# Letting the transposing DMAs run ahead, and two small reorderings, in a layer norm + (S5 state space ∥ SwiGLU) kernel

## The chip, the cores and the metric

One core of one Trainium2 chip. The metric is the device time of one execution in microseconds; each kernel was run several times, and for two kernels that are compared, in alternation on the same chip. The profile gives a span that is about 1.8 us shorter than the metric.

## The reference

The input x has 2048 tokens of 512 elements. All tensors are bf16.

```python
xn = (x - mean(x)) / sqrt(var(x) + 1e-5)                 # over the 512 elements
# S5: a diagonal complex state space over the 2048 tokens
dt = exp(log_dt); Lam = Lambda_re + 1j*Lambda_im; Lam_bar = exp(dt*Lam)
Bu = xn @ (((Lam_bar - 1)/Lam)[:, None] * (B_re + 1j*B_im)).T
h[t] = Lam_bar * h[t-1] + Bu[t]
ssm = 2*real(h @ (C_re + 1j*C_im).T) + xn*Dskip
# SwiGLU, 512 -> 1376 -> 512
ffn = (silu(xn @ w_gate) * (xn @ w_up)) @ w_down
out = x + ssm + ffn
```

## The kernel before

The work is cut into 4 chunks of 512 tokens; a chunk is 4 x tiles of 128 tokens. Chunk 0 is x tiles 0 to 3, chunk 1 is 4 to 7, chunk 2 is 8 to 11, chunk 3 is 12 to 15.

The program first builds a list of tasks with what each reads and writes, and then orders them. TensorE and SP (SyncE, which issues most DMAs) keep the order in which the tasks were added. The orders of ScalarE, VectorE and GpSimd are chosen by a list scheduler before the program is built, from *estimated* durations, and are fixed from then on. Whatever changes an estimated time in the plan can therefore change these three orders, and at run time an engine waits for the next task of its list even if a later one is ready.

```python
_CHAIN = ("pe", "sp")        # in program order; the other engines are ordered by the scheduler
# ... (cut)
# in _schedule: the estimated times of a DMA
        if t.dma:
            issue_done = st + t.est
            xs = max(st + min(t.est, 300.0), dma_free[e])
            dma_free[e] = xs + t.nbytes / (_DMA_BW if e == "sp" else 0.5 * _DMA_BW)
            t.fin = dma_free[e] + _DMA_LAT
            free[e] = issue_done
```

A transposing DMA waits for all DMAs before it, and every later DMA waits for the last transposing one:

```python
        def dma(name, dst, src, writes, nbytes, reads=(), after=(), out_=False, eng="sp", xpose=False, prio=0.0, order=(), **kw):
            after = tuple(after)
            if xpose:
                after = after + tuple(dma_tasks)
                # ... (cut)
            else:
                if xp_state[0] is not None:
                    after = after + (xp_state[0],)
                # ... (cut)

        x_load(0)
        x_load(1)
        act_q = [dma("ld_touch", tch[0:16], wg_v[0:128:8, :, 0:2], [("tch",)], 16 * 16, eng="act")]
        act_q.append(wg_load("a0", 0, 2, eng="act", order=(act_q[-1],)))
        x_load(2)
        act_q.append(wg_load("a1", 2, 3, eng="act", order=(act_q[-1],)))
        wg_load("a2", 3, 4)
        x_load(3)
        pload("ld_ldt", 2, A_log_dt)
        pload("ld_lim", 1, A_Lambda_im)
        pload("ld_lre", 0, A_Lambda_re)
        # ... (cut: w_up, the rest of w_gate, x tiles 4 to 7)
        # later on SP: ld_bre, ld_bim (transposing), the transposes of the normalised x (transposing),
        # ld_cre, ld_cim (transposing), then ld_x8 (x tiles 8 to 11), w_down, ld_x12, ld_dsk
```

The statistics of chunk 2 need x tiles 8 to 11 and go through three engines in four steps: VectorE's `bn_stats` and `bn_aggr`, GpSimd's power for `rstd`, VectorE's `nmr` (mean times rstd, negated), and ScalarE's normalisation `xn8` to `xn11`:

```python
        def ln_apply_act(a0):
            g.add("dve", ... nmr = -mv * rstd ..., name="nmr%d" % a0, est=70)
            for a in range(a0, a0 + 4):
                g.add("act", ... activation(out=xn_sb[:, a % NXN, :], in_=x_sb[:, a, :], func=AF.Identity,
                      scale=rstd[:, a:a + 1], bias=nmr[:, a:a + 1]), name="xn%d" % a, est=710)
```

The same ScalarE also evacuates TensorE's results from PSUM (`u_sb`, `sg`, `uf` in the profile); a bank pair that it hasn't emptied is one that TensorE can't write. VectorE computes, among much else, the C weights `W12` (`W` in the profile) that TensorE needs for the output of chunk 0.

## Time and profile before

Median 179.93 us (179.9 to 180.0, 6 runs). TensorE is nearly always busy:

| what | before | view |
|---|---|---|
| TensorE (PE) busy | 174.4 of 178.1 us, 98% | page |
| VectorE (DVE) busy | 162.3 us, 91% | page |
| ScalarE (ACT) busy | 88.8 us, 50% | page |
| TensorE's longest row without a gap | 7.01 us to 175.77 us | timeline |
| x tiles 8 to 11: issued, landed | 36.79, 40.26 us | timeline and trace |
| last C weight ready, first needed | 73.08, 75.06 us | timeline |

From the page of the kernel before (its lines on busy time and on the chain of work that ended last, by engine and by line):

```profile
span 178.1 us, 2421 instructions
PE 174.4 (98%) x929; PEld 84.1 (47%) x937; DVE 162.3 (91%) x281; ACT 88.8 (50%) x114; POOL 10.3 (6%) x21
...
PE 95%; DVE 2%; DMA 1%; issue 0%; ACT 0%
```

The chain is 95% TensorE: nothing but its own row of matmuls sets the time after start-up. SP's timeline of the kernel before (start us, duration us, then what is issued; the duration is that of the issue, not of the transfer):

```profile
5.81 0.55 SPq L400 DMA_DIRECT2D x_sb<-in_A_x_dram  x1
14.00 2.06 SPq L395 DMA_TRANSPOSE BT<-in_A_B_re_dram  x1
18.54 2.00 SPq L395 DMA_TRANSPOSE BT<-in_A_B_im_dram  x1
22.90 1.78 SPq L395 DMA_TRANSPOSE xnT<-xn_sb  x1
28.54 1.70 SPq L395 DMA_TRANSPOSE hss<-in_A_C_re_dram  x1
32.63 1.97 SPq L395 DMA_TRANSPOSE hss<-in_A_C_im_dram  x1
36.79 0.37 SPq L400 DMA_DIRECT2D x_sb<-in_A_x_dram  x1
```

The gaps between the transposes, 14.00 to 18.54 and so on, are the waits: each starts only when the one before has landed. The first line is x tiles 4 to 7, the last x tiles 8 to 11. The gate weights are issued on ScalarE's queue, behind the touch DMA; its timeline has

```profile
1.23 0.97 ACTq L400 DMA_DIRECT2D wg<-in_B_w_gate_dram  x2
```

What then happens to x tiles 8 to 11 is read from VectorE's timeline, then ScalarE's, then TensorE's (a bracket gives the idle time before an instruction and what ended it):

```profile
40.28 2.47 DVE L479 BATCH_NORM_STATS2 st<-x_sb 128x6 f32<-128x512 bf16 x4 [0.76 <-DMA x_sb<-in_A_x_dram]
...
45.67 0.16 DVE L500 SCALAR_TENSOR_TENSOR nmr<-mv,rstd 128x4 f32<-128x4 f32 x1 [0.86 <-POOL rstd L491]
```
```profile
43.88 1.02 ACT L754 ACTIVATE sg<-pb 128x1024 bf16<-128x1024 f32 x1
45.95 2.93 ACT L503 ACTIVATE xn_sb<-x_sb,nmr,rstd 128x512 bf16<-128x512 bf16 x4 [1.04 <-DVE nmr L500]
48.78 1.00 ACT L810 ACTIVATE uf<-pb 128x1024 bf16<-128x1024 f32 x1
```

### The profile page before, as it was taken

The numbers are of one execution on the slowest core, as the hardware profiler recorded it, in microseconds if no ns is written. First come the engines' busy times: TensorE is split into PE (matmuls) and PEld (weight loads), VectorE is DVE, ScalarE is ACT, GpSimd is POOL, SyncE is SP. The second block draws the span as 40 slices with busy tenths as digits, with TensorE's granted clock in tenths as the row PEclk, the third lists the DMA queues.
The fourth block names the chain that finished last, engine by engine and source line by source line (L and its number), as shares of the span: only waits on it lengthen the run. The fifth ranks groups of instructions, "written<-read, shape, count | busy, mean of one in ns | idle before, by whom it ended". The sixth has DMA issues, their size and how long they took to land.

```text
span 178.1 us, 2421 instructions
## 1 busy us (share of the span) xinstructions
PE 174.4 (98%) x929; PEld 84.1 (47%) x937; DVE 162.3 (91%) x281; ACT 88.8 (50%) x114; POOL 10.3 (6%) x21
## 2 busy tenths in 40 slices
PE   8999999999999999999999999999999999999994
PEld 2794444444444444444444444444444444444743
DVE  2958984889799999989999999999999999999983
ACT  4469999999799948016565651000965620000000
POOL 3023300002200000050000000000000000000000
PEclk9999999999999999999999999999999999999999
DMA  5995593669260000001330000001100000000123
GB/s 168 377 328 117 119 118 74 136 179 346 88 121 0 0 0 0 0 31 61 86 64 0 0 0 4 0 0 59 59 0 4 0 0 0 0 0 4 59 77 100
DMA packets 22978, 12.37 MB, mean 69 GB/s; under 512 B 15192, under 2 KB 22968, under 8 KB 22968
## 3 DMA queue, kind: packets, MB, share of 16 engines
q1 hardware_dynamic: 22472, 11.54, 24.9%
q10 hardware_dynamic: 496, 0.69, 1.1%
q8 instruction: 7, 0.11, 0.3%
q14 instruction: 3, 0.02, 0.0%
HBM read 6.46 MB, written 2.10 MB: 48 GB/s over the span
## 4 chain that ended last, share of the span: by engine, by line
PE 95%; DVE 2%; DMA 1%; issue 0%; ACT 0%
PE pb L742 36%; PE pb L940 21%; PE pb L857 16%; PE pb L953 15%; PE pb L783 3%; PE pb L820 2%; DMA x_sb<-in_A_x_dram 1%; PE pb L830 1%; PE pb L568 1%; DVE xn_sb L514 1%; DVE st L527 0%; DVE st L509 0%; ACT sd L521 0%; DVE mv L519 0%; DVE rstd L530 0%
## 5 line engine op out<-in xcount | busy, mean ns | idle before, releaser
L897 DVE TENSOR_TENSOR_SCAN rot<-sm,car,rot 128x512 bf16<-128x512 f32 x32 | 38.9, 1266 | 0.1
L940 PE MATMUL pb<-wd,hT 128*128 128x512 bf16 (+3 forms) x194 | 38.1, 355 | 0.2
L742 PE MATMUL pb<-xnT,wu 128*128 128x512 bf16 x160 | 37.3, 379 | 0.0
L742 PE MATMUL pb<-xnT,wg 128*128 128x512 bf16 x132 | 31.3, 379 | 0.0
L953 PE MATMUL pb<-W,hss 128*128 128x512 bf16 (+2 forms) x140 | 28.1, 355 | 0.2
L857 PE MATMUL pb<-xnT,BT 128*128 128x512 bf16 x128 | 28.1, 379 | 0.0
L940 PEld LDWEIGHTS pb<-wd,hT 128*128 128x128 bf16 (+1 forms) x198 | 18.5, 98 | 19.9
L742 PEld LDWEIGHTS pb<-xnT,wu 128*128 128x128 bf16 x160 | 15.6, 98 | 18.9 <-issue 0.2
L754 ACT ACTIVATE sg<-pb 128x1024 bf16<-128x1024 f32 x20 | 20.2, 1025 | 8.3 <-PE pb L742 7.2
L810 ACT ACTIVATE uf<-pb 128x1024 bf16<-128x1024 f32 x20 | 20.6, 1029 | 6.8 <-PE pb L742 6.7
L953 PEld LDWEIGHTS pb<-W,hss 128*128 128x128 bf16 x144 | 13.4, 98 | 14.3
L742 PEld LDWEIGHTS pb<-xnT,wg 128*128 128x128 bf16 x132 | 12.7, 98 | 15.7 <-issue 0.8
L857 PEld LDWEIGHTS pb<-xnT,BT 128*128 128x128 bf16 x128 | 12.5, 98 | 15.1
L864 ACT ACTIVATE u_sb<-pb 128x1024 bf16<-128x1024 f32 x16 | 16.4, 1027 | 4.6 <-PE pb L857 4.2
L812 DVE TENSOR_TENSOR hT<-sg,uf 128x1024 bf16<-128x1024 bf16 x20 | 13.5, 682 | 0.8 <-ACT uf L810 0.6
L888 DVE TENSOR_TENSOR rot<-u_sb,cosT 128x2048 bf16<-128x2048 bf16 x8 | 9.7, 1218 | 2.9 <-ACT cosT L703 2.9
L958 DVE TENSOR_TENSOR x_sb<-pb,x_sb 128x512 bf16<-128x512 f32 (+2 forms) x18 | 10.8, 622 | 1.2 <-PE pb L953 1.2
L839 ACT ACTIVATE sg<-pb 96x1024 bf16<-96x1024 f32 x2 | 2.0, 1021 | 17.3 <-PE pb L820 17.3
L503 ACT ACTIVATE xn_sb<-x_sb,nmr,rstd 128x512 bf16<-128x512 bf16 x8 | 5.9, 803 | 9.6 <-DVE nmr L500 9.6
L888 DVE TENSOR_TENSOR rot<-rot,cosT 128x2048 bf16<-128x2048 bf16 x8 | 9.7, 1215 | 0.1
L888 DVE TENSOR_TENSOR rot<-rot,sin 128x2048 bf16<-128x2048 bf16 x8 | 9.7, 1216 | 0.0
L888 DVE TENSOR_TENSOR rot<-u_sb,sin 128x2048 bf16<-128x2048 bf16 x8 | 9.7, 1216 | 0.0
(78 smaller groups left out, 144.3 us busy)
## 6 DMA issues: line engine op xcount, KB each, us to landing
out_dram<-x_sb SPq DMA_DIRECT2D x15, 128.0 KB, 1.7
x_sb<-in_A_x_dram SPq DMA_DIRECT2D x3, 512.0 KB, 7.6
wd<-in_B_w_down_dram SPq DMA_DIRECT2D x1, 1280.0 KB, 7.1
wu<-in_B_w_up_dram SPq DMA_DIRECT2D x1, 768.0 KB, 5.0
wu<-in_B_w_up_dram SPq DMA_DIRECT2D x1, 608.0 KB, 7.1
x_sb<-in_A_x_dram SPq DMA_DIRECT2D x4, 128.0 KB, 3.3
wg<-in_B_w_gate_dram SPq DMA_DIRECT2D x1, 480.0 KB, 6.0
wg<-in_B_w_gate_dram ACTq DMA_DIRECT2D x1, 448.0 KB, 3.8
```

The lines of the kernel that those rows point to most:

```text
L503: g.add("act", lambda e, a=a: e.activation(out=xn_sb[:, a % NXN, :], in_=x_sb[:, a, :], func=AF.Identity, scale=rstd[:, a:a + 1], bias=nmr ...
L742: inst = e.matmul(pbank[0:fs, bk, :].rearrange("p (j t) -> p j t", j=4), lhsT=w[:, kt, i * 128:i * 128 + fs], rhs=xnT[:, c % 2, :, kt, :], ...
L754: g.add("act", lambda e: e.activation(out=sg[rows, sl, 0:n, :].rearrange("p a t -> p (a t)"), in_=pair_f32(rows, bk, 512 * n), func=AF.Sil ...
L810: g.add("act", lambda e: e.activation(out=uf[rows, ul, 0:n, :].rearrange("p a t -> p (a t)"), in_=pair_f32(rows, bk, 512 * n), func=AF.Ide ...
L812: g.add("dve", lambda e: e.tensor_tensor(out=hT[rows, hb, i0:i0 + n, :], in0=sg[rows, sl, 0:n, :], in1=uf[rows, ul, 0:n, :], op=ALU.mult), ...
L857: inst = e.matmul(pbank[:, bk, :].rearrange("p (j t) -> p j t", j=4), lhsT=BT[:, ri, kt, pt * 128:(pt + 1) * 128], rhs=xnT[:, c % 2, :, kt ...
L864: g.add("act", lambda e: e.activation(out=u_sb[:, us].rearrange("p r t -> p (r t)"), in_=pair_f32(slice(0, 128), b0), func=AF.Identity), r ...
L888: tt = lambda out, a, b, op, r, w, nm: g.add("dve", lambda e: e.tensor_tensor(out=out, in0=a, in1=b, op=op), reads=r, writes=w, name="%s_% ...
L897: g.add("dve", lambda e, A0=A0, A1=A1, k=k, ri=ri, pt=pt: e.tensor_tensor_scan(out=A1[:, k, ri, :], data0=rr[:, pt:pt + 1].to_broadcast([1 ...
L940: inst = e.matmul(pbank[:, bk, 0:nc_], lhsT=hT[0:fs, hb, i, lt * 128:(lt + 1) * 128], rhs=wd[0:fs, i, c0:c0 + nc_], start=(i == 0), stop=F ...
L953: inst = e.matmul(pbank[:, bk, 0:nc_], lhsT=hss[:, hb, pt, ri, lt * 128:(lt + 1) * 128], rhs=W12[:, ri, pt, c0:c0 + nc_], start=False, sto ...
L958: g.add("dve", lambda e, bk=bk, a=a, c0=c0, nc_=nc_: e.tensor_tensor(out=x_sb[:, a, c0:c0 + nc_], in0=pbank[:, bk, 0:nc_], in1=x_sb[:, a, ...
```

## The change

Three parts, each meant to start work earlier.

1. Transposing DMAs lose their waits. All are issued by SP, so they stay on one queue.
2. On ScalarE's queue the tiny touch DMA goes, and two parameter loads from SP's queue come in its place, ahead of the gate weights. (`act_table` also loses a bias operand.)
3. On VectorE, the statistics of tile 1's first half come ahead of tile 0's reciprocal.

```diff
@@ transposing DMAs
             if xpose:
-                after = after + tuple(dma_tasks)
 ...
-                if xp_state[0] is not None:
-                    after = after + (xp_state[0],)
@@ ScalarE's queue
-        act_q = [dma("ld_touch", tch[0:16], wg_v[0:128:8, :, 0:2], [("tch",)], 16 * 16, eng="act")]
+        act_q = [pload("ld_ldt", 2, A_log_dt, eng="act")]
+        act_q.append(pload("ld_lim", 1, A_Lambda_im, eng="act", order=(act_q[-1],)))
         act_q.append(wg_load("a0", 0, 2, eng="act", order=(act_q[-1],)))
 ...
-        pload("ld_ldt", 2, A_log_dt)
-        pload("ld_lim", 1, A_Lambda_im)
@@ VectorE, chunk 0
             last = ln_stat0(0, (bn_full(0),))
+            last = bn_half(1, 0, order=(last,))
             for a in range(4):
                 # reciprocal of tile a, first half of tile a ...
-                if a == 0:
-                    last = bn_half(1, 0, order=(last,))
-                    last = ln_half(0, 1, order=(last,))
 ...
-                if a:
-                    last = ln_half(a, 1, order=(last,))
+                last = ln_half(a, 1, order=(last,))
```

(The removal of the now unused names and of `bias=epst[:, 0:1]` in `act_table` is cut.)

More of the change, by code (lines that the diff above doesn't have):

```diff
@@ L331, in bass_parallel_sum__ssm_conv_s5__swiglu_ffn__prompt_kernel @@
         epst = sb("epst", [128, 1], F32)
-        tch = sb("tch", [16, KT, 2], B16)
         praw = sb("praw", [128, 3, PT], B16)
@@ L386, in bass_parallel_sum__ssm_conv_s5__swiglu_ffn__prompt_kernel @@
         wu_v = B_w_up.rearrange("(k p) f -> p k f", p=128)
-        dma_tasks = []
-        xp_state = [None]
         def dma(name, dst, src, writes, nbytes, reads=(), after=(), out_=False, eng="sp", xpose=False, prio=0.0, order=(), **kw):
@@ L402, in dma @@
             t = g.add(eng, fn, reads=reads, writes=writes, name=name, dma=True, after=after, out=out_, est=est, nbytes=nb, prio=prio, order=order)
-            dma_tasks.append(t)
-            if xpose:
-                xp_state[0] = t
             return t
@@ L462, in act_table @@
         def act_table(func, order):
-            g.add("act", lambda e: e.activation(out=sm[:, NSM - 1, 0:1], in_=epst[:], func=func, bias=epst[:, 0:1]), reads=[("epst",)], writes=[("sm", "_warm")],
+            g.add("act", lambda e: e.activation(out=sm[:, NSM - 1, 0:1], in_=epst[:], func=func), reads=[("epst",)], writes=[("sm", "_warm")],
                   name="act_warm", est=1500, order=order)
```

## The prediction

> **What bounds the kernel.** The chain of waits that ended last is 95% TensorE. From 7.01 us to 175.77 us it is one row of matmuls with 0.05 us pauses; the windows table gives TensorE 17.00 of 17.00 us busy in most stretches at a granted clock of 1.00. Before that come about 6.2 us of start-up (first x tile's DMA 0.79 to 3.04, statistics, square root on ScalarE, reciprocal, normalisation of tiles 0 and 1), after it about 2 us of last addition and store. Only the start-up can be shortened, unless a new wait opens later.
>
> **What the change does.**
> 1. Transposing DMAs lose their waits. In the timeline of the DMA queue the B transposes start at 14.0 and 18.54 us, xnT of chunk 1 at 22.9, the C pair at 28.54 and 32.63, x tiles 8 to 11 at 36.79. Each issue takes about 2.0 us and lands 4.1 to 4.5 us after its start; its data flow about 2.2 us. I expect B issued from about 6 us, xnT at about 19.5 (it waits for VectorE), x tiles 8 to 11 at about 25, landed near 29.6 instead of 40.2. All stay on one queue: the Trainium skill, "DMA: Bandwidth & Descriptors", section "Silent corruption: two transposing streams in flight at once", asks for waits only between streams; no run here shows it yet. TensorE reads B first at 24.75 us, 1.85 us after it lands already: no gain. VectorE recovers part of its 4.1 us idle between 25 and 41 us (statistics of chunk 2 fill the 2.85 us wait for the cosine table).
> 2. The 0.41 us touch DMA on ScalarE's queue gives way to two parameter loads (0.37 and 0.25 us on SP). Gate weights and the table load (2.23 us) move about 0.3 us later; the first square root had 0.19 us of slack, so it starts about 0.1 us late. SP gets free about 0.7 us earlier; its loads are limited by bandwidth, so little follows.
> 3. Tile 1's first statistics (0.42 us) move into the 0.36 us in which VectorE waits for the square root. But x tile 1 lands near 4.2 us by the issue table (issued 1.24, about 2.95 us), after the 3.97 us at which it could start; so tile 0's reciprocal slips about 0.1 us. Tile 1's comes about 0.25 us earlier, and the first transpose of tile 1 (now 7.01 us) 0.1 to 0.2 us earlier.
>
> **Sum.** About -0.15 us of 179.94: predicted 179.8 us, 8 in 10 between 179.5 and 180.2. Faster by over 2%: 0.01; within 2%: 0.97; slower: 0.02.
>
> **What would show it.** TensorE's unbroken row starts 0.1 to 0.2 us earlier; B transposes issued near 6 us, landed by 18; VectorE idle in 25 to 41 us cut by over 2 us; TensorE busy time unchanged; hss of the last chunk, now finished at 168.35, finished 2 to 3 us earlier.
>
> **What would make it wrong.** (a) The new VectorE order puts a residual addition and chunk 3's statistics (about 3.6 us) ahead of the C weights W. W ends at 73.0, TensorE needs it at 75.06; I estimate 73.7 to 74, but if x tiles 8 to 11 land after 31 us, TensorE waits up to 1 us. (b) ScalarE waits for chunk 2's statistics amid PSUM evacuations; about 1.4 us of slack. (c) Transposes beside the w_up load delay it past 14.38 us.

## More of the kernel before

```profile
40.38 1.05 PE L830 MATMUL pb<-xnT,wu 128*64 128x512 bf16 x8
41.37 1.90 PE L742 MATMUL pb<-xnT,wg 128*128 128x512 bf16 x8
...
44.83 1.89 PE L742 MATMUL pb<-xnT,wg 128*128 128x512 bf16 x8
...
75.06 5.13 PE L953 MATMUL pb<-W,hss 128*128 128x512 bf16 x22
```

ScalarE waits 1.04 us for `nmr` and then runs four normalisations before its next evacuation, at 48.78; TensorE shows no gap around it. So one wait of about 1 us was already in ScalarE's list and cost nothing.

## The result

| | us, median | range, runs | ratio to before, 95% |
|---|---|---|---|
| before | 179.93 | 179.9 to 180.0, 6 | |
| after | 181.91 | 181.2 to 184.24, 6 | 1.0096 [1.0078, 1.0115] |

The run of 184.24 was slow (clock 0.991) and is left out of the ratio. A ratio here is the mean time of one kernel's fast runs over the mean of the other's fast runs of the same rounds, so it isn't quite the ratio of the medians. The change costs 1%, and the prediction's range (179.5 to 180.2) didn't hold it.

The page of the kernel after, the same lines:

```profile
span 180.1 us, 2416 instructions
PE 175.4 (97%) x937; PEld 84.2 (47%) x937; DVE 161.9 (90%) x281; ACT 87.9 (49%) x114; POOL 10.0 (6%) x21
...
PE 73%; DMA 8%; SPq 6%; DVE 6%; ACT 4%; POOL 2%; issue 1%; ACTq 0%; DVEq 0%
```

The busy times hardly moved. (TensorE's 1 us more is not made of the 8 matmul records that the profile before lacks, 929 against 937: e12 below has all 937, with 174.4 us.) But the chain now passes through a DMA, SP's queue, VectorE, GpSimd and ScalarE before it comes back to TensorE. ScalarE's queue, then SP's timeline, after:

```profile
1.67 0.96 ACTq L394 DMA_DIRECT2D wg<-in_B_w_gate_dram  x2
```
```profile
5.16 1.28 SPq L394 DMA_DIRECT2D x_sb<-in_A_x_dram  x1
6.48 7.72 SPq L391 DMA_TRANSPOSE BT<-in_A_B_re_dram  x1
14.24 3.03 SPq L391 DMA_TRANSPOSE BT<-in_A_B_im_dram  x1
20.16 1.81 SPq L391 DMA_TRANSPOSE xnT<-xn_sb  x1
22.01 2.64 SPq L391 DMA_TRANSPOSE hss<-in_A_C_re_dram  x1
24.69 3.59 SPq L391 DMA_TRANSPOSE hss<-in_A_C_im_dram  x1
28.32 0.58 SPq L394 DMA_DIRECT2D x_sb<-in_A_x_dram  x1
```

Two things to see. The gate weights on ScalarE's queue start 0.44 us later. And x tiles 8 to 11 are issued 8.5 us earlier, but not as early as hoped, since the issues themselves have become long: 7.72, 3.03, 2.64 and 3.59 us where each took 1.7 to 2.1 us before. They landed at 32.74 us (issue to landing 4.4 us). VectorE, ScalarE and TensorE after:

```profile
32.77 2.47 DVE L469 BATCH_NORM_STATS2 st<-x_sb 128x6 f32<-128x512 bf16 x4 [3.65 <-DMA x_sb<-in_A_x_dram]
...
38.76 0.16 DVE L490 SCALAR_TENSOR_TENSOR nmr<-mv,rstd 128x4 f32<-128x4 f32 x1 [1.00 <-POOL rstd L481]
```
```profile
39.01 0.81 ACT L493 ACTIVATE xn_sb<-x_sb,nmr,rstd 128x512 bf16<-128x512 bf16 x1 [4.23 <-DVE nmr L490]
39.73 1.00 ACT L851 ACTIVATE u_sb<-pb 128x1024 bf16<-128x1024 f32 x1
40.63 0.80 ACT L493 ACTIVATE xn_sb<-x_sb,nmr,rstd 128x512 bf16<-128x512 bf16 x1
```
```profile
40.78 1.05 PE L817 MATMUL pb<-xnT,wu 128*64 128x512 bf16 x8 [0.16 <-ACT u_sb L851]
42.40 1.90 PE L729 MATMUL pb<-xnT,wg 128*128 128x512 bf16 x8 [0.56 <-ACT u_sb L851]
...
46.66 1.90 PE L729 MATMUL pb<-xnT,wg 128*128 128x512 bf16 x8 [0.63 <-ACT uf L828]
...
77.04 3.19 PE L940 MATMUL pb<-W,hss 128*128 128x512 bf16 x14
```

The statistics of chunk 2 are now 7.5 us earlier, and yet ScalarE waits four times as long for them, 4.23 us instead of 1.04. The scheduler, which expected x tiles 8 to 11 even earlier (its plan, read by building the kernels again without a chip, has them land at 28.34 us; before, at 38.41), put the normalisations at a much earlier place in ScalarE's list: between the evacuations of `u_sb`. While ScalarE waits for `nmr`, it evacuates nothing, and TensorE runs out of PSUM. Comparing starts of the same matmuls before and after:

| matmul row | before | after | lag | added |
|---|---|---|---|---|
| w_up, 64 wide | 40.38 | 40.78 | 0.40 | 0.23 |
| w_gate | 41.37 | 42.40 | 1.03 | 0.63 |
| w_gate, two rows on | 44.83 | 46.66 | 1.83 | 0.80 |
| first use of W | 75.06 | 77.04 | 1.98 | 0.15 |

The lag at 38.5 us, before the first row of the table, is 0.17 us and comes from start-up (below). The next three rows add 1.67 us (unrounded), the wait for W another 0.15. Their sum, 1.99 us, is the growth of the span (178.1 to 180.1).

The start-up: TensorE begins tile 1's w_gate matmuls at 7.44 us instead of 7.13, because it waits 0.3 us for a part of the gate weights; by 13.5 us 0.17 us of that is left. This is one profile's start: the same first DMAs gave other starts in other runs (see below).

```profile
PEld pb L729 <- ACT u_sb L851: 1.2, 2, 1.0
PEld pb L729 <- ACT uf L828: 1.1, 1, 1.1
...
PEld pb L940 <- DVE W L704: 0.5, 1, 0.5
...
PEld pb L770 <- DMA wg<-in_B_w_gate_dram: 0.3, 1, 0.3
```

These are from the waits view of the kernel after, for TensorE's weight loads (in total, times, longest). None of the four is in the same view of the kernel before.

### The profile page after: what moved, and what is told of

The parts are those of the page before. It is cut to its first block, busy times and chain, and to the rows that moved or that the text cites. A ratio compares the mean times of both kernels' runs of the same rounds, so it can differ in the third digit from the quotient of the medians.

```text
span 180.1 us, 2416 instructions
## 1 busy us (share of the span) xinstructions
PE 175.4 (97%) x937; PEld 84.2 (47%) x937; DVE 161.9 (90%) x281; ACT 87.9 (49%) x114; POOL 10.0 (6%) x21
## 4 chain that ended last, share of the span: by engine, by line
PE 73%; DMA 8%; SPq 6%; DVE 6%; ACT 4%; POOL 2%; issue 1%; ACTq 0%; DVEq 0%
PE pb L729 27%; PE pb L927 21%; PE pb L940 15%; PE pb L844 8%; DMA x_sb<-in_A_x_dram 8%; SPq L391 4%; DVE st L469 3%; SPq L394 2%; ACT xn_sb L493 2%; ACT u_sb L851 2%; POOL rstd L481 1%; PE pb L807 1%; DVE xn_sb L485 1%; DVE hT L799 1%; POOL ve L477 1%
## 5 line engine op out<-in xcount | busy, mean ns | idle before, releaser
L927 PE MATMUL pb<-wd,hT 128*128 128x512 bf16 (+3 forms) x198 | 38.8, 355 | 0.0
L940 PEld LDWEIGHTS pb<-W,hss 128*128 128x128 bf16 x144 | 13.4, 98 | 14.5 <-DVE W L704 0.5
L469 DVE BATCH_NORM_STATS2 st<-x_sb 128x6 f32<-128x512 bf16 x12 | 7.5, 680 | 5.4 <-DMA x_sb<-in_A_x_dram 5.4
```

Source lines behind the costliest of these rows:

```text
L469: return g.add("dve", lambda e, a=a: e.bn_stats(out=st[:, a, :], in_=x_sb[:, a, :]), reads=[("x", a)], writes=[("st", a)], name="bnst%d" % ...
L927: inst = e.matmul(pbank[:, bk, 0:nc_], lhsT=hT[0:fs, hb, i, lt * 128:(lt + 1) * 128], rhs=wd[0:fs, i, c0:c0 + nc_], start=(i == 0), stop=F ...
L940: inst = e.matmul(pbank[:, bk, 0:nc_], lhsT=hss[:, hb, pt, ri, lt * 128:(lt + 1) * 128], rhs=W12[:, ri, pt, c0:c0 + nc_], start=False, sto ...
```

## The experiments

The theory: **the cost is ScalarE's fixed order**. The scheduler planned for x tiles 8 to 11 earlier than they land; ScalarE waits for them in front of evacuations that TensorE needs. The rivals: (R1) the unserialized transposes cost by themselves, by contention or by SP's long issues; (R2) the start-up, that is the later gate weights, costs it all; (R3) VectorE's later C weights W cost it. And, once the place was known: does the *lateness* of the loads cost the time, or the *order* that was made for it?

All 14 experiments gave correct results. The ratio is to the kernel before in the same rounds.

### e1 to e3: each part alone

**e1_transposes_only**: before, with part 1.

```diff
-                after = after + tuple(dma_tasks)
-                if xp_state[0] is not None:
-                    after = after + (xp_state[0],)
```

> Before with nothing but the waits of the transposing DMAs taken away; the scheduler then orders VectorE and ScalarE anew. Theory A (the loss between 38 and 77 us comes with this part, because the new order puts chunk 2's normalisation between PSUM evacuations and x tiles 8 to 11 land too late for it): 180.7 to 181.7 us, x tiles 8 to 11 landing near 32 us, ScalarE waiting 2 to 4 us for nmr, TensorE's start-up unchanged at 7.01 us. Rival (the loss belongs to the start-up parts, whose later loads push everything): within 0.2 us of before.

Measured: 179.91 us, 1.0009 [0.9997, 1.0022]. **A miss** for theory A. ScalarE waits 1.68 us for `nmr` (statistics at 31.79), and none of it reaches TensorE: the waits view shows 0.4 us of TensorE's weight loads on ScalarE, but its matmuls after the wait are as late against the kernel before as those ahead of it (0.06 us).

**e2_ploads_only**: before, with part 2, apart from the bias.

```diff
-        act_q = [dma("ld_touch", ..., eng="act")]
+        act_q = [pload("ld_ldt", 2, A_log_dt, eng="act")]
+        act_q.append(pload("ld_lim", 1, A_Lambda_im, eng="act", order=(act_q[-1],)))
...
-        pload("ld_ldt", 2, A_log_dt)
-        pload("ld_lim", 1, A_Lambda_im)
```

> Before with only the two parameter loads in place of the touch DMA on ScalarE's queue. Theory: gate weights are issued 0.44 us later and the second gate load lands near 7.4 us instead of 5.9, so TensorE waits about 0.3 us for it: 180.1 to 180.3 us. Rival (the start-up loss of the changed kernel comes from VectorE's new order instead): within 0.05 us of before.

Measured: 181.38 us, 1.0082 [1.0069, 1.0095], **a miss** upwards. The smallest part makes most of the loss. x tiles 4 to 7 land near 14.5 us instead of 13.76; the serialized chain behind them shifts (B_re's issue 14.90 instead of 14.00, x tiles 8 to 11 37.97 instead of 36.79); chunk 2's statistics start at 41.56 instead of 40.28, ScalarE waits 2.27 us for `nmr` instead of 1.04, and TensorE waits 0.9 us for the evacuation of `uf` behind it:

```profile
47.26 2.93 ACT L501 ACTIVATE xn_sb<-x_sb,nmr,rstd 128x512 bf16<-128x512 bf16 x4 [2.27 <-DVE nmr L498]
```
```profile
PE pb L740 <- ACT uf L808: 0.9, 1, 0.9
```

From there on TensorE is 1.07 us later than ahead of the wait, against the kernel before; near the end it loses 0.42 us more, waiting for `hss`. ScalarE's order is that of the kernel before; its wait is 1.23 us longer because the statistics come 1.28 us later.

**e3_stats_only**: before, with part 3 (its diff is the last block of the change).

> Before with only the statistics of tile 1 ahead of tile 0's reciprocal. Theory: first transpose of tile 1 at about 6.85 instead of 7.01 us and every later matmul earlier by as much: 179.7 to 179.85 us. Rival (x tile 1 lands too late, about 4.2 us, and holds the reciprocal): 179.95 to 180.2 us.

Measured: 179.99 us, 1.0 [0.9988, 1.0013]. Tile 1's first transpose starts at 6.95 instead of 7.01 us, as part 3 intends, but ScalarE's wait grows to 1.65 us and TensorE waits 0.3 us for `uf`. So the theory's range was **missed**; the time lies in the rival's, but not for the rival's reason.

What follows: R1 falls, the transposes alone cost nothing. Part 2 is the trigger. In e2 the wait is the same one (ScalarE, `nmr`, then an evacuation) in the serialized arrangement, so it doesn't need part 1.

### e4 and e6: the order and the DMAs of part 1, taken apart

In e4 the kernel after issues its DMAs as it does, but the scheduler orders the engines as if the old waits were there. e6 is the reverse: the kernel after's order, with the old waits at run time.

```diff
+            # extra: the waits of the kernel before for this DMA
+            xtra.append((t, extra))
...
+        for t, x in xtra:          # e4 only: plan with the old waits
+            t.deps |= x
         streams = _schedule(g.tasks, engs)
+        for t, x in xtra:          # e4: run without them    (e6: t.deps |= x, run with them)
+            t.deps -= x
```

> The changed kernel, whose DMA waits stay away on the chip, but whose engines' order is made with the old waits in the scheduler's graph, so VectorE and ScalarE keep the old order in chunk 0. Theory A (the compute order causes the loss): TensorE waits nowhere between 14 and 77 us, only the start-up loss of 0.17 us is left: 180.0 to 180.3 us. Rival B (transposing DMAs in flight beside loads hurt by themselves): 181.3 us or more.

Measured: 179.86 us, 0.9996 [0.9984, 1.0008]. The DMAs run as in the kernel after (x tiles 8 to 11 issued at 28.36 us), and ScalarE doesn't wait for `nmr` at all: its normalisations stand late in its list, at 44.82 us, in the order of the kernel before. The expected start-up loss of 0.17 us isn't there (0.02), so the time is below its range.

> The changed kernel's order on every engine, but on the chip the transposing DMAs wait as before. Theory (the landing of x tiles 8 to 11 decides): it lands near 41.5 us instead of 32.7, ScalarE waits 12 to 13 us for nmr, and about 8.5 us more of it reach TensorE: 188 to 191 us. Rival (transposes in flight together cost the time by themselves): 180 to 181 us, as they wait again.

Measured: 190.27 us, 1.0569 [1.0519, 1.0619] (profile at a clock of 0.982). ScalarE waits 13.00 us for `nmr` and TensorE 8.9 us for ScalarE. ScalarE's line, then TensorE's wait:

```profile
47.40 0.81 ACT L501 ACTIVATE xn_sb<-x_sb,nmr,rstd 128x512 bf16<-128x512 bf16 x1 [13.00 <-DVE nmr L498]
```
```profile
PE pb L825 <- ACT u_sb L859: 8.9, 1, 8.9
```

What follows: the same DMAs with another order lose nothing (e4); the same order with later DMAs loses 8.4 us more than the kernel after (e6). The mechanism is shown, and R2 falls: e4 keeps the changed start of the DMAs, part 2's too, and is as fast as before.

### e5: the late input earlier

The kernel after with x tiles 8 to 11 issued ahead of the two C transposes; the orders of the other engines stay.

```diff
         streams = _schedule(g.tasks, engs)
+        q = streams["sp"]
+        x8 = next(t for t in q if t.name == "ld_x8")
+        q.remove(x8)
+        q.insert(next(k for k, t in enumerate(q) if t.name == "ld_cre"), x8)
```

> The changed kernel, every engine's order as it is, but the load of x tiles 8 to 11 is issued ahead of the two C transposes. Theory (ScalarE holds PSUM while it waits for chunk 2's statistics, whose load lands at 32.7 us in the changed kernel): the load lands at 26 to 27 us, ScalarE's wait for nmr falls from 4.23 us to under 1, TensorE waits nowhere between 14 and 80 us, only the start-up loss is left: 180.0 to 180.2 us. Rival (the order of ScalarE by itself, normalisation between evacuations, costs it, on time or not): 181.3 us or more.

Measured: 179.64 us, 0.9977 [0.9935, 1.0019]. The statistics start at 29.04, ScalarE waits 0.93 us where it waited 4.23, W is ready at 73.26:

```profile
35.27 0.82 ACT L493 ACTIVATE xn_sb<-x_sb,nmr,rstd 128x512 bf16<-128x512 bf16 x1 [0.93 <-DVE nmr L490]
```

The whole loss is gone with one DMA moved. The time is below the expected range, as the start-up loss is missing here too. It isn't shown to beat the kernel before: the interval holds 1. (The intervals of e5 to e8 are wide because one run of the kernel before in these rounds, at a clock of 0.991, took 182.26 us and counts as fast. Without it the ratios would be about 0.12% higher.)

### e7: part 2 taken back

```diff
-        act_q = [pload("ld_ldt", 2, A_log_dt, eng="act")]
-        act_q.append(pload("ld_lim", 1, A_Lambda_im, eng="act", order=(act_q[-1],)))
+        act_q = [dma("ld_touch", ..., eng="act")]
...
+        pload("ld_ldt", 2, A_log_dt)
+        pload("ld_lim", 1, A_Lambda_im)
```

> The changed kernel with the touch DMA on ScalarE's queue and the parameter loads on SP again, so the change without its middle part; its ScalarE order is that of the first experiment, normalisation one evacuation later than in the changed kernel. Theory: x tiles 8 to 11 land near 31.8 us, ScalarE waits about 1.7 us, TensorE 0 to 0.4 us, start-up 0.1 us better than before: 179.8 to 180.1 us. Rival (unserialized transposes plus the new statistics order suffice for the loss): 181 us or more.

Measured: 179.88 us, 0.9989 [0.9948, 1.0029]. Without part 2 the rest costs nothing. Tile 1's first transpose starts at 6.76 us, 0.25 us earlier than before: that is the gain that the prediction expected of part 3. The kernel after, at 7.07, didn't get it in its profile; but e4, e5, e6, e8 and e13, which start with the same DMAs as it does, have 6.77 to 6.89, so part 2 doesn't take this gain away.

### e8: ScalarE's places alone

The kernel after with chunk 2's normalisations one evacuation later in ScalarE's list. This makes ScalarE's list the same as e7's from there on.

```diff
+        q = streams["act"]
+        # tm3 to just before uev_b1_1; xn8 .. xn11 each behind the next evacuation
```

> The changed kernel, DMAs untouched, but on ScalarE the four normalisations of chunk 2 stand one evacuation later (a table step moves up into the place), as in the first experiment's order. Theory (slot and landing together make the wait): ScalarE waits about 2.5 us instead of 4.23, TensorE 0 to 0.3 us instead of 1.67: 180.0 to 180.5 us. Rival (the late data cost the same wherever ScalarE asks for them): 181.3 us or more.

Measured: 181.91 us, 1.0079 [1.0033, 1.0125]: **a miss.** The wait moved:

```profile
PE pb L940 <- DVE W L704: 1.5, 1, 1.5
...
PE pb L729 <- ACT uf L828: 0.4, 1, 0.4
```

TensorE hardly waits for ScalarE now, but 1.5 us for VectorE's W. R3 isn't false, then: it is a second path by which the same late input reaches TensorE, and it had been hidden in the kernel after because TensorE was already late when it came to W.

### e9 to e12: other ways to arrange the same loads

e9: the two parameter loads behind the gate weights on ScalarE's queue, no touch DMA. e10: e9 with e5's edit. e11: e7 with e5's edit. e12: e2 with x tiles 8 to 11 ahead of the C transposes, order kept.

```diff
 e9
-        act_q = [pload("ld_ldt", ...), pload("ld_lim", ...)]   (shortened)
-        act_q.append(wg_load("a0", 0, 2, eng="act", order=(act_q[-1],)))
+        act_q = [wg_load("a0", 0, 2, eng="act")]
...
+        act_q.append(pload("ld_ldt", ...)); act_q.append(pload("ld_lim", ...))   (behind a1)
```

> The changed kernel with the two parameter loads behind the gate weights on ScalarE's queue instead of ahead of them (no touch DMA); ScalarE's compute order is the changed kernel's. Theory (the parameter loads cost by making the gate weights start late, which moves every later load): gate weights issued near 0.8 us, x tiles 4 to 7 landed by 13.8 instead of 14.5, x tiles 8 to 11 near 31.5 instead of 32.7, ScalarE's wait for nmr 2.5 to 3.5 us: 179.7 to 180.6 us. Rival (a first DMA on ScalarE's queue is needed as a warm-up, or the parameter loads hurt wherever they stand): 181.2 us or more.

Measured: 181.82 us, 1.0095 [1.0073, 1.0117]: **a miss.** With nothing in front of the gate weights on ScalarE's queue, x tiles 0 and 1 on SP's land late: at 3.36 and 5.00 us instead of 3.04 and 4.11, though issued as before. VectorE's timeline in e9 (a clock of 0.991):

```profile
3.39 0.69 DVE L517 BATCH_NORM_STATS2 st<-x_sb 128x6 f32<-128x512 bf16 x1 [3.39 <-DMA x_sb<-in_A_x_dram]
4.11 0.18 DVE L509 BATCH_NORM_AGGREGATE mv<-st 128x2 f32<-128x6 f32 x1
5.03 0.43 DVE L499 BATCH_NORM_STATS2 st<-x_sb 128x6 f32<-128x256 bf16 x1 [0.73 <-DMA x_sb<-in_A_x_dram]
5.37 0.15 DVE L521 RECIPROCAL rstd<-sd 128x1 f32<-128x1 f32 x1
```

Tile 0's statistics start at 3.39 us (before: 3.07), tile 1's wait until 5.03, and by part 3's order tile 0's reciprocal comes behind them, at 5.37 instead of 4.34. TensorE waits 1.7 us at the start, and is 2.22 us late when the start-up is over. What the theory said of ScalarE came true: its wait for `nmr` falls to 2.50 us and costs TensorE nothing; W costs 0.19 us.

> The same, with the load of x tiles 8 to 11 ahead of the C transposes as well. Theory: no wait of TensorE after the start-up, and a start-up at least as good as in the statistics-only kernel: 179.3 to 179.7 us, the fastest so far.

Measured: 182.02 us, 1.0088 [1.0052, 1.0123]: **a miss** for the same reason. ScalarE and W cause no wait here; the first use of BT is at 26.83 us instead of 24.75, and that 2.1 us of start-up is all the growth of its span (180.2).

> The touch-back kernel (touch DMA, parameter loads on SP, unserialized transposes, statistics order) with x tiles 8 to 11 loaded ahead of the C transposes. Theory: no wait left but the start-up, which is 0.1 to 0.2 us better than before: 179.5 to 179.8 us, with less spread between runs than touch-back alone (179.47 to 180.68).

Measured: 179.7 us, 0.9989 [0.9974, 1.0004].

> The parameter-loads-only kernel, with its order and its serialized transposes, but x tiles 8 to 11 loaded right after chunk 1's transpose, ahead of the C transposes. Theory (that kernel lost 1.5 us because x tiles 8 to 11 landed at 41.5 us instead of 40.2): ScalarE's wait for nmr falls from 2.27 us to 0, only the start-up loss of 0.1 us is left: 179.9 to 180.2 us. Rival (the parameter loads cost 1.5 us by something else): 181.2 us or more.

Measured: 179.92 us, 0.9998 [0.9985, 1.001], where e2 had 1.0082. Statistics at 38.19 instead of 41.56, and no wait of ScalarE for `nmr`. In the serialized arrangement too, earlier x tiles 8 to 11 cure what part 2 costs.

### e13 and e14: order against lateness

e8 left open how the loss divides: part 2 makes the loads land later *and* makes the scheduler choose other orders. Both e13 and e14 move whole orders. e13 has the DMAs of the kernel after, with e7's lists of ScalarE and VectorE. e14 has e7's DMAs, with the lists of the kernel after.

```diff
         streams = _schedule(g.tasks, engs)
+        # ScalarE: the moves of e8 (e13), or their reverse (e14)
+        VORD = ("...").split()      # the other kernel's order of VectorE's 281 tasks
+        streams["dve"].sort(key=lambda t: VORD.index(t.name))
```

> The changed kernel's DMAs, with ScalarE's and VectorE's static orders copied from e7 (the changed kernel with the touch DMA back). If the loss comes mainly from the orders that part 2 made the scheduler choose (chunk 2's normalisations one evacuation earlier, table steps later on VectorE): 179.9 to 180.5 us, VectorE's W by 75.5 us, no wait of TensorE for W. If it comes from the loads being 0.7 to 1.5 us later, whatever the order: 181.3 to 182 us, as the changed kernel.

> The mirror: e7's DMAs (touch DMA in front, the two parameter loads on SP's queue), with ScalarE's and VectorE's orders of the changed kernel. Orders to blame: 181.0 to 182 us, ScalarE waiting about 2.9 us for chunk 2's nmr and W at about 76.5 us. Lateness to blame: 179.8 to 180.3 us.

| | e7's orders | the changed kernel's orders |
|---|---|---|
| touch DMA in front (loads earlier) | e7: 179.88 us, 0.9989 [0.9948, 1.0029] | e14: 180.56 us, 1.0047 [1.0021, 1.0072] |
| parameter loads in front (loads later) | e13: 180.13 us, 1.0025 [0.9996, 1.0055] | after: 181.91 us, 1.0096 [1.0078, 1.0115] |

e13 came in the expected range (though TensorE still waits 0.3 us for W), e14 **missed** its own: it lies between. So both count. How they share the loss can't be said from these ratios: the four come from three sets of rounds, and e7's carries the run of 182.26 us. The profiles, with each start-up taken off (how much later TensorE's rows come than in the kernel before, after 80 us less at 30 us), have a loss of 0.00 us in e7, 0.43 in e13, 0.83 in e14 and 1.82 in the kernel after: the two together cost more than the sum of each, because the first part of a wait is absorbed (see below). The two aren't quite apart, either: in e13 chunk 2's statistics start at 32.20, between e7's 31.43 and the 32.77 of the kernel after, since x tiles 8 to 11, issued at the same time as in the kernel after, landed 0.57 us sooner; why isn't shown.

These runs also show why W came late in e8. VectorE, from the start of chunk 2's statistics to the end of the last W, is idle only for 1.0 us (the wait for GpSimd's `rstd`) in all the kernels of the next table. So W is ready a fixed time after x tiles 8 to 11, and the fixed time depends on the order alone:

| VectorE's order | kernel | statistics start | last W ends | difference |
|---|---|---|---|---|
| of the changed kernel | after | 32.77 | 76.98 | 44.22 |
| | e5 | 29.04 | 73.26 | 44.23 |
| | e8 | 32.97 | 77.14 | 44.17 |
| | e14 | 31.43 | 75.67 | 44.24 |
| of e7 | e7 | 31.43 | 74.37 | 42.94 |
| | e13 | 32.20 | 75.12 | 42.92 |
| of e1 | e1 | 31.79 | 74.74 | 42.94 |

The changed order has one statistics instruction of chunk 3 more in this stretch (about 0.6 us of the 1.3), and runs six table steps for the sine one by one, where e7's runs them in pairs that overlap (3.0 us in the kernel after, 2.6 in e13). A late load and a longer stretch add up, and W is needed at 75.06 us plus whatever TensorE has lost by then.

## Why the prediction was wrong

What it had right. TensorE bounds the kernel; its busy time hardly changed (174.4 and 175.4 us). B landed earlier and gave nothing. The transposes together in flight on one queue did no harm: every run was correct, as the Trainium skill has it ("DMA: Bandwidth & Descriptors", section "Silent corruption: two transposing streams in flight at once", which asks for a wait between streams and not within one). What (c) feared didn't happen: the later w_up load landed at 12.92 us. And both mechanisms of the loss were on its list of what would make it wrong: (a) W late if x tiles 8 to 11 land after 31 us, (b) ScalarE waiting for chunk 2's statistics amid evacuations. They landed at 32.74.

What failed, term by term:

1. **"x tiles 8 to 11 at about 25, landed near 29.6 instead of 40.2."** This is the step that failed. Measured: issued at 28.32, landed at 32.74. The landing took 4.4 us from the issue (4.6 by the estimate); the issue was 3.3 us late. Of that, 0.66 us is the start of the transpose of chunk 1's xn (20.16 instead of 19.5), which follows x tiles 4 to 7 that landed 0.7 us later. Most of the rest, 2.2 us, is the C transposes: I took about 2 us for each issue, from the serialized kernel (the scheduler has the same figure, 2000 ns). Unserialized they took 2.64 and 3.59. The four long issues of the kernel after end 0.1 to 0.5 us before the DMA ahead of them on the queue lands (B_re's at 14.20, x tiles 4 to 7 at 14.47; B_im's at 17.27, B_re at 17.70; C_re's at 24.65, xnT at 24.80; C_im's at 28.28, C_re at 28.76). In e5, where x tiles 8 to 11 stand in front, C_re's issue takes 3.79 us and ends at 27.11, their landing being at 27.33. So removing the wait moved it into the issue: SP stands in the transposing DMA until the one ahead of it has nearly landed, and what stands behind it on SP, the plain load of x tiles, waits too. The traces of all eleven kernels without the waits have 44 such pairs, all with 0.09 to 0.62 us between the two times. The nearest to a test is e12: its only transpose issued behind an unfinished load, C_re's, took 2.85 us against 2.01 in e2 and ended 0.3 us before that load landed. No run was made for this alone, so what makes the issue long isn't shown.
2. **"Gate weights and the table load move about 0.3 us later ... little follows."** They start 0.44 us later, and a good deal follows: x tiles 4 to 7 land at 14.47 us instead of 13.76, and everything that hangs on those is late. (In the other profiles with the two loads in front they land at 14.23 to 14.88 us, with the touch DMA in front at 13.73 to 13.97, but for e11's 14.45.) The start-up itself is no clear loss: the kernel after is 0.17 us late in its profile, but e4, e5, e6, e8 and e13, with the same first DMAs, lie between 0.02 us late and 0.30 early, so part 3's gain isn't lost to part 2. The plan makes the same mistake as I did: with part 2 it has x tiles 8 to 11 land 0.85 us earlier (28.34 us in the kernel after, 29.19 in e7), while on the chip they landed 1.34 us later (32.74, 31.40). I had costed the sequencer's time, and not the transfers' place in the shared DMA engines. The Trainium skill says where to look ("DMA: Bandwidth & Descriptors", section "Issuing engines are not separate DMA queues": DMAs of different engines "interleave with each other" on the same 16 engines), and this agrees: in e9, with the gate weights first on ScalarE's queue, x tile 1 on SP's queue took 3.75 us from issue to landing instead of 2.86. In the kernel after, the DMA engines moved 150 GB/s between 3 and 4 us, and 326 before.
3. **"About 1.4 us of slack" (b).** The slack wasn't what failed; the wait was. Taking from ScalarE's wait for `nmr` what TensorE's rows lose there (against the kernel before), the old place absorbs 1.2 us: e2 waits 2.27 us and loses 1.07, e3 1.65 and 0.45, both with ScalarE's order of the kernel before. The new place, between `u_sb` evacuations, absorbs more, 2.56 us: 4.23 became 1.67 in the kernel after, 3.25 became 0.68 in e14, 13.00 became 10.44 in e6, and e9's 2.50 became nothing. But ScalarE now asks for `nmr` 10.1 us earlier (34.77 instead of 44.91 us), and gets it only 6.9 us earlier (`nmr` starts at 38.76 instead of 45.67). The Trainium skill's "PSUM — Partial Sum Buffer", section "Engine vs sequencer instructions", calls the queues of ScalarE and VectorE "strict FIFO"; the traces agree, most plainly e6, where ScalarE stands 13.00 us in front of evacuations that TensorE waits 8.9 us for.
4. **The cost if (a) or (b) happened, "up to 1 us".** It was 1.8 us, since both came from one late load: 1.67 us by ScalarE, 0.15 by W. Remove the first alone and the second shows in full (e8, 1.5 us).

And the rest of what it said would show it right: VectorE's idle time between 25 and 41 us wasn't cut by 2 us, it grew. In these 16 us it was busy 11.89 us before and 11.06 after, because it now waits 3.65 us for the x tiles. The B transposes were issued at 6.48 and 14.24 us, the second landing at 19.3 and not by 18; `hss` of the last chunk was finished 0.3 us earlier, at 168.01, not 2 to 3.

What stays open: what makes the issue of a transposing DMA long behind an unfinished one; whether e5, e7 or e11 is a true gain of 0.1 to 0.2%, which the scatter of their runs hides; and how the loss divides between order and lateness.

## What to carry to other kernels

A static order is made for planned landing times, and a load that comes later than planned costs on *every* engine whose list has work on it: before letting the scheduler replan, compare the planned with the measured time of each load, and read how long each engine could wait at the place it gets: at ScalarE's new place a wait of up to 2.50 us cost TensorE nothing here (e9), and one beyond 2.56 us all of the excess (e14, e6). Taking a wait away can move it into the issue of the next DMA, so put the load that is needed first ahead of the long ones on its queue (e5, e12), which cured the loss here at once. And undo the parts one by one even when one of them looks too small to matter: with two 1 KB loads left where they were (e7), there was no loss.

## What the Trainium skill lacked or had wrong

- "DMA: Bandwidth & Descriptors", section "Issuing engines are not separate DMA queues", calls the time of the sequencer to initiate a DMA "usually small relative to the DMA itself". For a transposing DMA behind unfinished ones it wasn't: B_re's issue took 7.72 of the 11.2 us to its landing, C_im's 3.59 of 5.6; with an idle queue they took 2.06 of 4.5 and 1.97 of 4.1, which isn't small either. I found no page that says that a transposing DMA's issue gets longer when those ahead of it on the queue are unfinished, or by how much.
- The same page's "Rules for kernel authors" says of a transpose next to ordinary DMAs that it "needs nothing". For correctness every run here agrees; for time it isn't free, as the point above shows. (It says nothing of time.)
- No page says how much the start order of small and large loads on two queues matters: with part 2's two loads in front, the gate weights started 0.44 us later and x tiles 4 to 7 landed 0.7 us later, though their own issue had started 0.65 us earlier, and with nothing in front of the gate weights (e9) x tile 1's statistics started at 5.03 us; in the kernel after they started at 3.77.
